# Two edits to a planned transformer kernel: K staged in bf16 before it is spread, and the last chunk worked in halves

## The chip, the cores and the metric

The kernel runs on one core of one Trainium2 chip. The metric is device time in microseconds for one launch; lower is better.

## The reference

Two layers with the same weights, each an attention block and a feed-forward block, over one sequence of 2048 rows of 512 in bf16:

```python
x = x + _A_ref(_layernorm(x), A_wqkv, A_wo)      # attention
x = x + _B_ref(_layernorm(x), B_w1, B_w2)        # feed forward
x = x + _A_ref(_layernorm(x), A_wqkv, A_wo)
x = x + _B_ref(_layernorm(x), B_w1, B_w2)

# _A_ref: H = 32 heads of Dh = 16, window W = 256
qkv = x @ wqkv                                    # 512 -> 3 x 512
scores = einsum("bhqd,bhkd->bhqk", q, k) * Dh ** -0.5
mask = (idx[:, None] - idx[None, :] >= 0) & (idx[:, None] - idx[None, :] < W)
o = softmax(where(mask, scores, -1e9)) @ v
return o @ wo
# _B_ref: relu(x @ w1) @ w2, 512 -> 1792 -> 512
```

## The kernel before

The 2048 rows are worked in chunks of 512, four for each layer: steps k = 0 to 7 (`NSTEP` is 8), counted layer by layer, so that k = 7 is the last chunk of the second layer. For each step there is:

- `plan_qkv(k)`: normalise four blocks of 128 rows, turn them (a DMA transpose, in step 0 TensorE), then K and Q for four groups t of 8 heads, and V for four blocks of rows.
- `plan_attention(k)`: scores, exp on ScalarE, masks on VectorE or GpSimd, P times V on TensorE (tile `acc`), division on VectorE into `O`. It goes by `Unit`s. A whole unit is one t with all 512 queries (8 blocks of 64); its scores are made in five groups of 2048 columns over four row groups (`FULL`). A half unit has 256 queries (4 blocks), and three groups, the last of half the width (`HALF`). All scores share one PSUM tile `Sps`, so a group's scores wait for the exp of the group before. `HALVED` lists the steps that are worked in half units: (0,).
- `plan_rest(k)`: turn `O` (a DMA transpose, in the last step TensorE), multiply by `wo`, add the residual, normalise, turn, then W1 with ReLU into `hT` (14 tiles f) and W2 for four blocks of rows. In a step of `HALVED`, W1 runs for 256 columns at a time, and W2 of the first two blocks stands between the two halves. There is one `hT` and one `xn2T`, so W1 of a step waits for W2 of the step before.

K is kept "spread" in `KBD`: for each slot of 64 keys two copies, one with the even heads' rows and one with the odd heads' rows, the other rows zero. `spread_k` writes it with two operations, each multiplying by a column of `par` (0 or 1 by the parity of the row's head). `KBD` is a ring of 20 slots; a chunk of 8 slots that runs over the ring's end (steps 2 and 7) takes four operations. Before the change `spread_k` reads the PSUM tile of the projection, on VectorE or ScalarE. V takes another way: it is copied from PSUM to a bf16 staging tile `Vst`, one of three buffers of the pool `stg`, and spread into `V2` from there on GpSimd or VectorE. The output tiles `ob` use `stg` too.

The order of all work is made ahead of time by a planner in the kernel's own Python (lines 692 to 800). Every operation has a key, the engines that may run it, and a planned time for each. The planner walks through time; when an engine is idle it takes the ready operation with the lowest key (on TensorE) or the lowest ready time plus key (elsewhere), and an operation that needs a buffer waits until one is planned to be free. Scores have the lowest keys of all. Projections are keyed by the score group ahead of which they are wanted: `at = first_slot[...] - 16`, sixteen groups early. W1 and W2 have later keys and fill TensorE between score groups. Where nothing can run, the planner puts a `warm` matmul on TensorE whose result nobody uses. Each engine then runs its operations in exactly the planned order, whatever the real times are. Four PSUM buffers (`psum`) serve all projections, transposes and `acc`.

Every instruction goes through one helper, so all carry the same line number (L106) in the profile, and groups are told apart by tile names: `KBD`, `Vst`, `Sps`, `Pb` (the exponentials), `acc`, `ps_d` (projections), `hT`, `xn`, `OT`.

Of the kernel before, what the change touches and what calls it, by code (L numbers as in the profile page):

```python
# [10 lines left out]
BF16 = mybir.dt.bfloat16  # L11
I32 = mybir.dt.int32
AX = mybir.AxisListType
ACT = mybir.ActivationFunctionType
ALU = mybir.AluOpType
P = 128
# [46 lines left out]
def kernel(  # L63
# [19 lines left out]
    NSTEP = 2 * NCH  # L83
# [31 lines left out]
    pe, dve, act, pool, sp = (InOrder(x) for x in (nc.tensor, nc.vector, nc.scalar, nc.gpsimd, nc.sync))  # L115
# [38 lines left out]
    par = const.tile([P, 2], FP32, name="par")  # L154
# [31 lines left out]
    SOON = {"qkv": 0, "v": 0, "h": 0, "mask": 0, "div": -1, "add": -1}  # L186
# [34 lines left out]
    def op(key, opts, deps=(), take=None, uses=(), keep=0):  # L221
        uses = list(uses) + ([take] if take is not None and take not in uses else [])
        return Op(key, opts, deps, take, uses, keep)
# [3 lines left out]
    stg = Pool("stg", 3, work)  # L227
# [11 lines left out]
    d_wo, d_w1 = landed(18.0), landed(24.0)  # L239


    def copy(e, o, i, relu=False):
        if e == "ACT":
            act.activation(o, i, ACT.Relu if relu else ACT.Copy)
        elif e == "POOL":
            pool.tensor_copy(o, i)
        elif relu:
            dve.tensor_relu(o, i)
        else:
            dve.tensor_copy(o, i)  # L250

    EVAC = {512: {"DVE": 0.67, "ACT": 0.59}, 256: {"DVE": 0.42, "ACT": 0.38}}

    def options(times, fn):
        return {e: (t, lambda e=e: fn(e)) for e, t in times.items()}
# [67 lines left out]
    def spread_k(e, layer, c, t, h0, h1, ps):  # L323
        s0 = slot(layer, 8 * c)
        for a, b in ([(h0, h1)] if s0 + h1 <= NSLOT or s0 + h0 >= NSLOT else [(h0, NSLOT - s0), (NSLOT - s0, h1)]):
            sa = (s0 + a) % NSLOT
            for p in range(2):
                o = KBD[:, t, sa:sa + b - a, p, :]
                i = ps[:, 64 * a:64 * b].rearrange("p (s k) -> p s k", k=64)
                if e == "ACT":  # L330
                    act.activation(o, i, ACT.Copy, scale=par[:, p:p + 1])
                else:
                    dve.tensor_scalar(out=o, in0=i, scalar1=par[:, p:p + 1], scalar2=None, op0=ALU.mult)

    def spread_v(e, layer, c, j, src):
        v4 = src.rearrange("p (a e d) -> p e a d", e=2, d=16)
# [80 lines left out]
        dve.tensor_tensor(out=x_sb[:, b, :], in0=ps, in1=x_raw(b, b + 1)[:, 0, :] if raw else x_sb[:, b, :], op=ALU.add)  # L417


    HALVED = (0,)  # L420
    units, base = [], []
    for k in range(NSTEP):
        base.append(sum(len(u.groups) for u in units))
# [12 lines left out]
    c_par = op(-9, {"DVE": (0.5, parity)}, [c_pidx])  # L436
# [15 lines left out]
    k_done, q_done, v_done, qkv_mm, w1_mm, w2_mm, x_done = {}, {}, {}, {}, {}, {}, {}  # L452
# [8 lines left out]
    def plan_qkv(k):  # L461
        layer, c = divmod(k, NCH)
        xnTs[k] = xnT = [None]
        src = [x_raw(4 * c + j, 4 * c + j + 1)[:, 0, :] if layer == 0 else x_sb[:, 4 * c + j, :] for j in range(4)]
        lid = 2 * k
        st, dst = [], []
        calm = (-10, 1, 40, 60)[k] if k < 4 else 0
        for j in range(4):
            came = [d_x[j // 2] if c == 0 else d_xc[c]] if layer == 0 else [x_done[k - 4, j]]
            st.append(norm_stats(lid, j, src[j], came + applied.get(lid - 8, []), j - 1 if j % 2 else None, calm))  # L470
        pw = [norm_pow(lid, j, j + 2, [st[j], st[j + 1]], calm - 5) for j in (0, 2)]
        free = [] if k == 1 else qkv_mm.get(k - 1, []) + (qkv_mm[0] if k == 2 else [])

        class Late:
            def __getitem__(self, i):
                if xnT[0] is None:
                    xnT[0] = work.tile([P, KC, 512], BF16, name="xnT", tag="hT" if k == 1 else "xnT", bufs=1)
                return xnT[0]
        for j in range(4):
            dst.append(norm_apply(lid, j, src[j], [pw[j // 2]], k == 0, Late(), -5000, free))  # L480
        applied[lid] = list(dst)
        mine = qkv_mm[k] = []
        old = [scores[s] for n in units_of.get(k - 2, []) for s in range(first_slot[n], first_slot[n] + len(units[n].groups))]
        old_pv = [pvs[n, j] for n in units_of.get(k - 2, []) for j in range(units[n].nq // 2)]
        wait = 0 if k == 0 else 16
        for h in range(2) if k == 0 else (None,):
            cols = slice(0, 512) if h is None else slice(256 * h, 256 * h + 256)
            h0, h1 = (0, 8) if h is None else (4 * h, 4 * h + 4)
            us = 0.216 if h is None else 0.115
            need_x = dst if h is None else dst[2 * h:2 * h + 2]  # L490
            w = 512 if h is None else 256
            for t in range(4):
                at = first_slot[units_of[k][t + 4 * (h or 0)]] - wait
                idx = 4 * k + t

                def kmm(kc, ps, t=t, cols=cols):
                    mm(ps[:, cols], wqkv[:, kc, D + t * P:D + (t + 1) * P], xnT[0][:, kc, cols], kc == 0, kc == KC - 1)
                box, m = group(at, KC, us, kmm, need_x + [d_w[1]] + old[len(old) * t // 4:len(old) * (t + 1) // 4], lead=1000)
                times = {"DVE": 1.46, "ACT": 1.42} if h is None else {"DVE": 0.87, "ACT": 0.83}
                k_done[k, t, h or 0] = op(SOON["qkv"], options(times, lambda e, t=t, h0=h0, h1=h1, box=box:  # L500
                                                      spread_k(e, layer, c, t, h0, h1, box.ps)),
                                          [m, c_par], None, [box])

                def qmm(kc, ps, t=t, cols=cols):
                    mm(ps[:, cols], wqkv[:, kc, t * P:(t + 1) * P], xnT[0][:, kc, cols], kc == 0, kc == KC - 1)
                last_use = [scores[s] for n, u in enumerate(units) if 4 * u.k + u.t == idx - 7
                            for s in range(first_slot[n], first_slot[n] + len(u.groups))]
                box, m2 = group(at + 0.1, KC, us, qmm, need_x + [d_w[0]] + last_use, lead=1000)

                def qev(e, t=t, cols=cols, box=box, idx=idx):  # L510
                    q = first(Q, (k, t), lambda: work.tile([P, 512], BF16, name="Qt", tag=f"Q{idx % 7}", bufs=1))
                    copy(e, q[:, cols], box.ps[:, cols])
                q_done[k, t, h or 0] = op(SOON["qkv"], options(EVAC[w], qev), [m2], None, [box])
                mine += [m, m2]
        for j in range(4):
            at = first_slot[units_of[k][0]] + (1 + (8 if j > 1 else 0) if k == 0 else 1.6 * j - wait)

            def vmm(kc, ps, j=j):
                mm(ps[:], xnT[0][:, kc, j * P:(j + 1) * P], wqkv[:, kc, 2 * D:3 * D], kc == 0, kc == KC - 1)
            box, m = group(at + 0.2, KC, 0.216, vmm, ([dst[j]] if k == 0 else dst) + [d_w[2]] + old_pv, lead=1000)  # L520
            vs = Box(stg)

            def vev(e, box=box, vs=vs):
                vs.t = vs.tile([P, 512], BF16, "Vst")
                copy(e, vs.t[:], box.ps[:])
            ev = op(SOON["qkv"], options(EVAC[512], vev), [m], vs, [box, vs])
            v_done[k, j] = op(SOON["v"], options({"POOL": 1.72, "DVE": 1.42} if k else {"POOL": 1.72, "DVE": 1.42, "ACT": 1.48}, lambda e, j=j, vs=vs: spread_v(e, layer, c, j, vs.t[:])),
                              [ev] + c_v, None, [vs])
            mine.append(m)
# [58 lines left out]
    def plan_rest(k):  # L588
# [43 lines left out]
        w1_mm[k], w2_mm[k] = [], []  # L632
        for j0, j1 in ((0, 2), (2, 4)) if k in HALVED else ((0, 4),):
            if k in HALVED:
# [78 lines left out]
    started, score_end, idle_since, log = set(), [0.0], [1.9], []  # L713
    score_next = [0]

    by_name = {"PE": pe, "ACT": act, "DVE": dve, "POOL": pool, "SP": sp}

    def choose(e, t):
        best = None
        for at, o in ready[e]:  # L720
# [39 lines left out]
    while events and events[0][0] < 3000:  # L760
        t, _, o, e = heapq.heappop(events)
# [15 lines left out]
        for e in ENGINES:  # L777
            if busy[e] > t + 1e-9:
                continue
            o = choose(e, t)  # L780
# [4 lines left out]
            elif e == "PE" and done_ops[0] < len(ops) - 12:  # L785
                if t - idle_since[0] >= (0.4 if t > 20 else 0.0) and sum(1 for f, _ in psum.free if f <= t) > 1:
                    box = Box(psum)
# [85 lines left out]
    with tc.If(flag > 0):  # L873
# [13 lines left out]
        for layer in range(2):  # L887
            for c in range(NCH):
# [3 lines left out]
                for t in range(4):  # L892
                    q = work.tile([P, 512], BF16, name="Qt", tag=f"Q{t}", bufs=1)
                    Qts.append(q)
                    whole(KC, lambda kc, ps: mm(ps[:], wqkv[:, kc, t * P:(t + 1) * P], xnT[:, kc, :], kc == 0, kc == KC - 1),
                          lambda ps: nc.vector.tensor_copy(q[:], ps[:]))
                    whole(KC, lambda kc, ps: mm(ps[:], wqkv[:, kc, D + t * P:D + (t + 1) * P], xnT[:, kc, :], kc == 0, kc == KC - 1),
                          lambda ps: spread_k("DVE", layer, c, t, 0, 8, ps))
                for j in range(4):
                    whole(KC, lambda kc, ps: mm(ps[:], xnT[:, kc, j * P:(j + 1) * P], wqkv[:, kc, 2 * D:3 * D], kc == 0, kc == KC - 1),  # L900
                          lambda ps: spread_v("DVE", layer, c, j, ps[:]))
# [52 lines left out]
```

## Time and profile before

| | |
|---|---|
| median of 3 runs | 484.27 us (484.21 to 484.54) |
| the profiled execution | 484.21 us, span 482.5 us |
| granted TensorE clock | 1.000 |
| PE busy | 461.9 us, 5935 matmuls |
| DVE (VectorE) busy | 366.4 us |
| ACT (ScalarE) busy | 337.2 us |
| POOL (GpSimd) busy | 312.4 us |
| score matmuls / exps | 1472 / 160 |

The span runs from the first to the last instruction; the time of an execution has some 1.7 us around it. A busy TensorE is not one at its peak, since the ends of matmuls are modelled: where matmuls of 512 columns stand back to back, each is shown with a duration of 0.38 us, but one starts every 0.216 us. The starts are what to count by.

### The profile page before, as it was taken

How to read it: one execution, taken by the hardware profiler on the slowest of the kernel's cores; microseconds unless marked ns; L12 is line 12 of the kernel's file. 1: busy time of each engine (PE TensorE's matmuls, PEld its weight loads, DVE VectorE, ACT ScalarE, POOL GpSimd, SP SyncE). 2: the span in 40 equal slices, each digit the busy share in tenths (PEclk: the TensorE clock that was granted, in tenths of full speed). 3: DMA queues.
4: the chain of work that ended last, by engine and by line, in shares of the span. 5: the costliest groups of instructions: out<-in, count | busy, mean ns of one | idle time of the engine just before them, and what ended most of it. 6: DMA issues, size and time to landing. Idle time of an engine off the chain costs nothing.

```text
span 482.5 us, 14414 instructions
## 1 busy us (share of the span) xinstructions
PE 461.9 (96%) x5935; PEld 242.3 (50%) x5935; DVE 366.4 (76%) x960; ACT 337.2 (70%) x268; POOL 312.4 (65%) x708
## 2 busy tenths in 40 slices
PE   7889899998899999999999999999999999999995
PEld 3555556654445545554544554455555545554442
DVE  6989899858897789878989977898758876473101
ACT  3877877877777767876778877777876787735240
POOL 7778878768876778777878767677655566520000
PEclk9999999999999999999999999999999999999999
DMA  8770231004300142002311023020153002000101
GB/s 271 244 206 3 45 45 25 2 3 67 67 1 3 24 67 46 3 1 45 58 34 33 13 35 47 12 46 1 24 89 57 13 1 56 24 14 12 35 12 37
DMA packets 54649, 21.98 MB, mean 46 GB/s; under 512 B 46128, under 2 KB 54064, under 8 KB 54576
## 3 DMA queue, kind: packets, MB, share of 16 engines
q1 hardware_dynamic: 54576, 20.98, 19.8%
q8 instruction: 48, 0.79, 0.7%
q14 instruction: 25, 0.20, 0.2%
HBM read 7.86 MB, written 2.10 MB: 21 GB/s over the span
## 4 chain that ended last, share of the span: by engine, by line
PE 72%; DVE 10%; DMA 7%; POOL 6%; issue 2%; ACT 2%; DVEq 0%; ACTq 0%; POOLq 0%
PE ps_d L106 52%; PE acc L106 12%; PE Sps L106 8%; DMA OT<-O 4%; POOL Pb L106 3%; ACT Pb L106 2%; DVE KBD L106 1%; DVE st L106 1%; DMA xn2T<-xn 1%; DVE xn L106 1%; DVE Pb L106 1%; POOL xn L106 1%; DVE x_sb L106 1%; DVE V2f L106 1%; DMA xnT<-xn 1%
## 5 line engine op out<-in xcount | busy, mean ns | idle before, releaser
L106 ACT ACTIVATE Pb<-Sps 128x2048 bf16<-128x2048 f32 (+4 forms) x160 | 283.3, 1770 | 94.4 <-PE Sps L106 75.8
L106 POOL TENSOR_SCALAR_AFFINE_SELECT Pb<-Pb 64x256 bf16<-64x256 bf16 x518 | 222.9, 430 | 99.3 <-ACT Pb L106 77.4
L106 PE MATMUL ps_d<-xn2T,w 128*128 128x512 bf16 (+1 forms) x504 | 109.5, 356 | 1.2 <-DVE hT L106 0.9
L106 PE MATMUL ps_d<-w,hT 128*128 128x512 bf16 x448 | 109.0, 380 | 0.0
L106 PEld LDWEIGHTS <-Pb 128*128 128x128 bf16 x2880 | 83.5, 96 | 25.6 <-issue 8.6
L106 PE MATMUL acc<-V2f,Pb 128*128 128x34 bf16 x2880 | 90.1, 178 | 2.3 <-POOL Pb L106 1.3
L106 PE MATMUL ps_d<-xnT,wqkv 128*128 128x512 bf16 (+1 forms) x288 | 66.5, 356 | 2.2 <-DMA xnT<-xn 1.0
L106 PEld LDWEIGHTS <-w 128*128 128x128 bf16 x504 | 45.3, 97 | 44.7 <-issue 5.4
L106 PE MATMUL Sps<-Qt,KBD 32*128 32x192 bf16 (+4 forms) x1472 | 61.6, 252 | 2.8 <-ACT Pb L106 2.5
L106 PEld LDWEIGHTS <-hT 128*128 128x128 bf16 x448 | 40.3, 98 | 46.0 <-issue 3.6
L106 DVE TENSOR_TENSOR Pb<-Pb,tri 128x512 bf16<-128x512 bf16 (+1 forms) x136 | 58.8, 437 | 5.0 <-ACT Pb L106 4.6
L106 DVE TENSOR_SCALAR hT<-ps_d 128x512 bf16<-128x512 f32 (+1 forms) x74 | 45.8, 625 | 11.4 <-PE ps_d L106 10.9
L106 PEld LDWEIGHTS <-KBD 32*128 32x128 bf16 x1472 | 24.0, 92 | 51.7 <-issue 48.9
L106 DVE TENSOR_SCALAR KBD<-ps_d,par 128x256 bf16<-128x256 f32 (+1 forms) x82 | 45.5, 604 | 1.6 <-PE ps_d L106 1.5
L106 DVE BATCH_NORM_STATS2 st<-x_sb 128x6 f32<-128x512 f32 (+1 forms) x64 | 43.7, 683 | 0.9 <-DMA x_sb<-in_A_x_dram 0.6
L106 ACT ACTIVATE hT<-ps_d 128x512 bf16<-128x512 f32 (+1 forms) x52 | 28.4, 550 | 20.9 <-PE ps_d L106 19.4
L106 DVE TENSOR_TENSOR x_sb<-ps_d,x_sb 128x512 f32<-128x512 f32 x48 | 32.7, 684 | 13.0 <-PE ps_d L106 12.4
L106 DVE TENSOR_TENSOR O<-acc,chk 128x128 bf16<-128x128 f32 x128 | 37.3, 291 | 4.5 <-DMA OT<-O 0.2
L106 DVE RECIPROCAL chk<-acc 128x8 f32<-128x8 f32 x128 | 25.6, 200 | 17.7 <-PE acc L106 15.2
L106 PEld LDWEIGHTS <-wqkv 128*128 128x128 bf16 x288 | 25.7, 97 | 26.1 <-issue 4.0
L106 DVE TENSOR_TENSOR ob<-ps_d,x_sb 128x512 bf16<-128x512 f32 x16 | 11.0, 690 | 34.4 <-PE ps_d L106 34.3
L106 PE MATMUL ps_d<-wo,OT 128*128 128x512 bf16 x128 | 32.5, 380 | 3.9 <-DMA OT<-O 3.6
(55 smaller groups left out, 300.3 us busy)
## 6 DMA issues: line engine op xcount, KB each, us to landing
w<-in_B_w_dram SPq DMA_DIRECT2D x2, 1792.0 KB, 10.0
out_dram<-ob SPq DMA_DIRECT2D x16, 128.0 KB, 1.7
wqkv<-in_A_wqkv_dram SPq DMA_DIRECT2D x3, 512.0 KB, 7.0
x_sb<-in_A_x_dram SPq DMA_DIRECT2D x3, 512.0 KB, 8.9
x_sb<-in_A_x_dram SPq DMA_DIRECT2D x2, 256.0 KB, 2.9
wo<-in_A_wo_dram SPq DMA_DIRECT2D x1, 512.0 KB, 8.9
xnT<-xn SPq DMA_TRANSPOSE x28, 2.5
OT<-O SPq DMA_TRANSPOSE x28, 2.5
```

Source lines behind the costliest of these rows:

```text
L106: inst = fn(*a, **k)
```

## The change

Two edits. `HALVED` gets the last step, so the last chunk's attention is done in half units and its W1 and W2 in halves of 256 queries. And in steps 1 to 7 K is first copied from PSUM to a bf16 staging tile `Kst` of the pool `stg` (on VectorE or ScalarE), and spread into `KBD` from there, on VectorE or GpSimd, with planned times of 0.8 and 1.3 us. Step 0 still spreads K from PSUM in halves. The change's short description also names a later load of W2; the line that plans that load is the same in both kernels.

```diff
@@ spread_k
                 if e == "ACT":
                     act.activation(o, i, ACT.Copy, scale=par[:, p:p + 1])
                 else:
-                    dve.tensor_scalar(out=o, in0=i, scalar1=par[:, p:p + 1], scalar2=None, op0=ALU.mult)
+                    by_name[e].tensor_scalar(out=o, in0=i, scalar1=par[:, p:p + 1], scalar2=None, op0=ALU.mult)
...
-    HALVED = (0,)
+    HALVED = (0, NSTEP - 1)
...
                 times = {"DVE": 1.46, "ACT": 1.42} if h is None else {"DVE": 0.87, "ACT": 0.83}
-                k_done[k, t, h or 0] = op(SOON["qkv"], options(times, lambda e, t=t, h0=h0, h1=h1, box=box:
-                                                      spread_k(e, layer, c, t, h0, h1, box.ps)),
-                                          [m, c_par], None, [box])
+                if k == 0:
+                    k_done[k, t, h or 0] = op(SOON["qkv"], options(times, lambda e, t=t, h0=h0, h1=h1, box=box:
+                                                                   spread_k(e, layer, c, t, h0, h1, box.ps[:])),
+                                              [m, c_par], None, [box])
+                else:
+                    ks = Box(stg)
+
+                    def kev(e, box=box, ks=ks):
+                        ks.t = ks.tile([P, 512], BF16, "Kst")
+                        copy(e, ks.t[:], box.ps[:])
+                    ev = op(SOON["qkv"], options(EVAC[512], kev), [m], ks, [box, ks])
+                    k_done[k, t, 0] = op(SOON["qkv"], options({"DVE": 0.8, "POOL": 1.3}, lambda e, t=t, ks=ks:
+                                                              spread_k(e, layer, c, t, 0, 8, ks.t[:])),
+                                         [ev, c_par], None, [ks])
```

The table `by_name` (engine name to engine) moves up so that `spread_k` can use it. A fallback path that did not run here gets a matching edit.

More of the change, by code (lines that the diff above doesn't have):

```diff
@@ L239 @@
     d_wo, d_w1 = landed(18.0), landed(24.0)
+    by_name = {"PE": pe, "ACT": act, "DVE": dve, "POOL": pool, "SP": sp}
     def copy(e, o, i, relu=False):
@@ L714 @@
     score_next = [0]
-    by_name = {"PE": pe, "ACT": act, "DVE": dve, "POOL": pool, "SP": sp}
     def choose(e, t):
@@ L897 @@
                     whole(KC, lambda kc, ps: mm(ps[:], wqkv[:, kc, D + t * P:D + (t + 1) * P], xnT[:, kc, :], kc == 0, kc == KC - 1),
-                          lambda ps: spread_k("DVE", layer, c, t, 0, 8, ps))
+                          lambda ps: spread_k("DVE", layer, c, t, 0, 8, ps[:]))
                 for j in range(4):
```

## The prediction

> **What bounds it now.** I read the page's parts 1 and 2 first, then busy time by stage, then the chain of waits, then the groups by shape.
>
> ```profile
> PE 461.9 (96%) x5935; PEld 242.3 (50%) x5935; DVE 366.4 (76%) x960; ACT 337.2 (70%) x268; POOL 312.4 (65%) x708
> ...
> core 0: us, PE busy (x) PEld busy (x) DVE busy (x) ACT busy (x) POOL busy (x), PEclk, DMA share, GB/s
> 24.00:104.00 80.00, 75.79 (x1156) 45.50 (x1157) 70.36 (x196) 62.41 (x52) 62.98 (x144) 1.00 0.22 50
> 104.00:126.00 22.00, 19.47 (x267) 9.82 (x264) 18.07 (x54) 16.15 (x11) 17.32 (x40) 1.00 0.30 50
> 126.00:400.00 274.00, 269.60 (x3726) 138.70 (x3723) 228.49 (x577) 208.58 (x144) 196.24 (x448) 1.00 0.18 31
> 400.00:428.00 28.00, 28.00 (x391) 15.13 (x388) 15.69 (x46) 19.05 (x15) 15.94 (x35) 1.00 0.16 40
> 428.00:453.00 25.00, 25.00 (x130) 11.86 (x129) 10.96 (x27) 8.85 (x15) 1.83 (x3) 1.00 0.05 17
> ```
>
> PE sets the end. From 126 us on it stands idle for only 4.4 us (274.00 less 269.60). Earlier it loses 4.2 us in 24 to 104 and 2.5 in 104 to 126, and it fills some of the rest with useless `warm` matmuls: 8 near 50 us, 8 in 104 to 126, at 0.216 us about 3.5 us in all. So about 10 us can be won before 126 us and about 4 after it; the rest is matmul time.
>
> The end of the chain shows why the last chunk has nothing to wait for:
>
> ```profile
> 443.10 34.33 PE ps_d L106 x159
> 477.43 0.02 issue
> 477.45 0.69 DVE ob L106
> ```
>
> 159 matmuls at 0.216 us stand back to back. The last attention matmul is at 426.1 us, and behind it lie most of W1 and all of W2 of chunk 6, then both for chunk 7.
>
> The one place where the K spread is on the chain:
>
> ```profile
> 108.23 1.56 DVE KBD L106 x4
> ...
> 110.62 1.56 DVE KBD L106 x4
> ...
> 113.68 3.90 DMA OT<-O
> 117.59 0.05 issue
> 117.63 1.05 PE ps_d L106 x4
> ```
>
> DVE spreads two K tiles of chunk 2 before the divisions whose result the transpose waits for, and PE then runs 5 warm matmuls and stands idle for 1.2 us. These are the prices:
>
> ```profile
> L106 DVE TENSOR_SCALAR KBD<-ps_d,par 128x512 bf16<-128x512 f32 x40 | 28.0, 741 | 0.9 <-PE ps_d L106 0.9
> L106 DVE CAST Vst<-ps_d 128x512 bf16<-128x512 f32 x18 | 12.3, 684 | 0.9 <-PE ps_d L106 0.7
> L106 ACT ACTIVATE Vst<-ps_d 128x512 bf16<-128x512 f32 x14 | 8.3, 595 | 0.5 <-PE ps_d L106 0.2
> L106 DVE TENSOR_SCALAR xn<-x_sb,mvs,rstds 128x512 bf16<-128x512 bf16 x10 | 4.2, 440 | 1.5 <-POOL rstds L106 1.5
> L106 POOL TENSOR_SCALAR xn<-x_sb,rstds,nbs 128x512 bf16<-128x512 bf16 x6 | 5.0, 836 | 0.6
> ```
>
> **The change, part by part.** The profiled execution took 484.21 us (span 482.5 and 1.7 around it), 0.06 below the median of 484.27, so I add to the median.
>
> *Scores of the last chunk.* A whole unit has five groups of 512 columns. Two half units have four of 512 and two of 256. In the chain a group of 8, 12 or 16 score matmuls of 512 columns takes 0.33 us, one of 4 takes 0.22 (at 41.96 us), and the ten matmuls ahead of a group take 2.26 instead of 2.16, so 0.10 more a group. That is 5 x 0.43 = 2.15 against 4 x 0.43 + 2 x 0.32 = 2.36: 0.21 for each of four t, **+0.84 us** on PE, which has no gap there to hide it.
>
> *W1 of the last chunk.* 112 matmuls of 256 columns replace 56 of 512. Chunk 0 already runs that shape: 14 in 1.54 us (62.00 to 63.54), 0.110 each. The 56 take 12.09 us (453.08 to 465.17); 112 x 0.110 = 12.32: **+0.2 us**. The 28 extra evictions (0.415 us on DVE, 0.381 on ACT) keep up: PE needs 0.44 us for each half tile and two engines share them. Nothing.
>
> *Earlier start of the first half: nothing.* Its W1 still waits for W2 of chunk 6 (one `hT`), and that ends at 453 us. Feed-forward work already fills PE during attention. The attention itself grows: a small group costs about 0.22 + 1.02 (its exp) + 0.37 of handover, 1.61, against 2.59 for a full one, so 2 x (2 x 2.59 + 1.61) = 13.6 against 13.0 us, 2.4 us for four t. What hides it: normalised rows are turned by 443 us and wanted at 453. Without that cover it would cost 2.4.
>
> *K, 28 tiles (chunks 1 to 7).* DVE pays 1.40 us a tile now (two of 0.741, 0.66 apart), 1.56 where the ring of slots wraps (four of 0.475). Afterwards: a copy (0.684 DVE or 0.595 ACT) and two spreads from bf16. No row shows such a spread. On DVE I take 0.44 each, the bf16 normalisation (its extremes are 0.384 and 0.578; the freest bf16 copy, half as wide, takes 0.22). On POOL 0.80, between 0.77 and 0.84. So DVE pays from nothing (ACT and POOL) to 1.56 (all DVE) a tile; at half and half 0.34 + 0.44 = 0.78, a gain of 0.6 or a little more. That is 17 us of DVE, but DVE isn't the bound after 126 us. On the chain it is worth 2 x 0.6 near 110 us; the ends are zero and the dry time of 104 to 126, 2.5 + 1.7 = 4.2. I take **-1.0**, since not all of PE's wait there is DVE's. A PSUM buffer comes free 0.7 us sooner; the waits for KBD that it could shorten are about 2 us, the most of them in that place or under it: nothing more. The scores want K sixteen groups later, so the longer way to KBD is covered; without that cover it adds about 1.5 us once a chunk.
>
> *POOL and the queues behind it.* The planner enters 1.3 us for a spread on POOL; I expect 1.6. What is queued behind it are masks, PV waits for the masks, and PE takes its work in order. 14 such spreads, 0.3 late each, are 4.2 us; POOL has 99 us of idle before masks, and PE's waits on POOL masks now total about 5 us. I take a quarter, **+1.0**; the ends are zero and 4.2. Every instruction after the first K copy of chunk 1 (31 us) is also ordered anew, so the 4.4 us of single waits after 126 are dealt again: 0, with 2 us either way. Three staging buffers now serve K as well as V: eight uses a chunk in place of four, each of a few us, in 30 us or more; nothing. W2's load, named in the description, isn't touched by the diff: nothing.
>
> Sum: +0.84 + 0.2 - 1.0 + 1.0 = **+1.0, 485.3 us**.
>
> A copy beside a busy POOL is the second thing that can shift these prices:
>
> ```profile
> L106 DVE COPY V2f<-Vst x64: 217/434/468, 13.2 to 382.5; 64x256 bf16<-64x256 bf16 x64
> L106 POOL COPY V2f<-Vst x64: 392/399/690, 14.5 to 381.4; 64x256 bf16<-64x256 bf16 x64
> ```
>
> The same DVE copy takes 217 ns at best and 434 at the median, and POOL's takes up to 690 against 399; the spread from PSUM stays between 717 and 751 ns. The Trainium skill ("SBUF — State Buffer", Who interferes with whom) says that a DVE instruction using both ports, SBUF to SBUF, and a GpSimd one exclude each other for their whole length; by that rule the new spread is exposed where the old was not, and the trace's doubled copies agree. By it some 28 spreads on DVE would each hold POOL or be held for about 0.2 us (434 less 217), 5.6 in all and a quarter of it at PE, and the sum would be 486.7 in place of 485.3. In "VectorE: DVE Perf Modes" (Rules for kernel authors) it advises copying PSUM to SBUF first where several operations follow; no run here shows whether two are enough.
>
> **Rivals.** *Relief on DVE is worth all of the dry time* (28%): spreads cost 0.22 to 0.3 us, or go to POOL without harm, and the transposes of O start 3 us earlier near 113 us. For: DVE is busy 88% in 24 to 104 and the chain runs through KBD. Against: POOL is at 79% there too and takes the work. It gives 484.3 + 1.0 - 4.2 = 481.1 at its end (without POOL's lateness), 482.2 in the middle.
> *POOL's masks come late* (25%): the 0.3 us of each spread, and exclusion beside DVE, reach PE through the masks. It decides from about half of the 14 spreads on, 2.1 us. At its end 484.3 + 1.0 + 4.2 = 489.5 without relief, 487.5 in the middle.
> *The planner gives POOL none* (5%): copy and spreads stay on DVE, 1.56 for 1.40; PE's +1.0 remains: 485.4.
> *The forecast* (42%): relief and lateness cancel, PE's +1.0 is left; 484.2 to 486.5.
>
> **Numbers.** A measurement of this kernel tells about 0.2% (0.97 us) from no change, so 483.3 to 485.2 is the same. Faster: the first rival, 0.28. Same: the lower half of the forecast's range and of the third rival, 0.24. Slower: the upper halves and the second rival, 0.48. The range for 8 in 10 leaves out the last of the relief and of the lateness: 481.3 to 488.6.
>
> **What would show it.** Sps matmuls rise from 1472 to 1536 and exps from 160 to 164; 224 W1 matmuls of 256 columns. 28 Kst copies, DVE spreads near 0.44 us, POOL's near 0.8. DVE busy falls by over 10 us, POOL's rises by some 20. PE stays back to back from 443 us to the end. I am wrong if that tail shows gaps, if idle before 126 us falls by 3 us or more, or if PE's waits on POOL masks double.

## The result, and the profile after

The changed kernel takes 492.63 us (median of four runs, 491.66 to 493.60) against 484.35 for the kernel before on the same chip: ratio 1.0171, 95% interval 1.015 to 1.0191. It is slower by 8.3 us, where 1.0 was forecast, and lies outside the range. The profiled execution took 491.66 us, with a span of 489.6 against 482.5.

Busy time by stage, in the same columns as for the kernel before:

```profile
24.00:104.00 80.00, 71.35 (x1043) 42.53 (x1044) 65.78 (x187) 58.61 (x50) 69.28 (x137) 0.98 0.22 49
104.00:126.00 22.00, 18.23 (x292) 9.89 (x289) 15.61 (x47) 16.60 (x10) 17.40 (x36) 1.00 0.28 38
126.00:400.00 274.00, 269.76 (x3689) 139.18 (x3689) 228.21 (x609) 210.24 (x152) 200.32 (x437) 1.00 0.19 32
```

Most of TensorE's added idle time lies in 24 to 104 us: PE stands idle for 8.65 us in place of 4.2, while POOL is busy for 69.3 in place of 63.0 and VectorE for 65.8 in place of 70.4. From 104 to 126 PE's idle time is 3.8 in place of 2.5. After 126 it did not grow (4.2 against 4.4), although POOL is busier there too (200.3 against 196.2), and PE stands back to back to the end as before. The mean clock of the first stage is 0.98.

One place holds most of it. The chain of waits there (start, duration, what):

```profile
51.75 6.47 POOL KBD L106 x4
58.21 0.70 POOL rstds L106
...
59.60 0.76 POOL xn L106
...
60.94 0.76 POOL xn L106
61.70 0.69 POOL rstds L106
62.39 0.03 issue
62.42 0.96 DVE xn L106 x2
63.37 0.34 DVE hT L106
63.71 0.04 issue
63.75 1.01 PE ps_d L106 x4
```

Four spreads, two K tiles of chunk 1, occupy POOL for 6.47 us where the plan has 2 x 1.3 = 2.6, so POOL is 3.9 us late behind them. Behind them in POOL's order stand the powers of two normalisations (`rstds`). VectorE's next operation in its order, a normalisation, waits for the second power; behind it stand the evictions of `hT`, and behind those a PSUM buffer that PE waits for. POOL, VectorE and TensorE stand in line behind the spreads. The list of waits puts it as (who <- for whom: us in total, times, longest):

```profile
DVE xn L106 <- POOL rstds L106: 6.8, 3, 5.3
...
PE ps_d L106 <- DVE hT L106: 4.4, 1, 4.4
```

The longest of each, 5.3 us of VectorE and 4.4 of PE, is this one. Right behind it the clock falls (the number before the last two is the granted TensorE clock):

```profile
62.00:64.00 2.00, 0.25 (x2) 0.18 (x2) 1.58 (x5) 0.00 (x0) 1.85 (x5) 0.91 0.47 91
64.00:66.00 2.00, 2.00 (x42) 1.45 (x40) 1.59 (x7) 0.00 (x0) 1.77 (x5) 0.50 0.58 111
66.00:68.00 2.00, 2.00 (x37) 1.68 (x30) 1.83 (x7) 1.73 (x1) 0.84 (x3) 0.74 0.47 94
```

The shares missing from full clock in the three rows, 0.09 x 2 + 0.50 x 2 + 0.26 x 2 = 1.7 us, are 3.4 us at half clock if the clock was half or full (the middle row has 0.50), and cost up to 1.7 us more. The account of the 7.1 us of span is then: 4.4 of idle before 104 us, 1.2 in 104 to 126, about 1.0 of added matmul time (an estimate from the prediction's rows), up to 1.7 for the clock, less about 0.65 since three warm matmuls fewer were made (35 for 38), and less 0.5 of idle before 24 us.

The new operations, by tile (min, median and max in ns):

```profile
L106 DVE TENSOR_SCALAR KBD<-Kst,par x48: 272/442/703, 43.7 to 398.7; 128x512 bf16<-128x512 bf16 x32, 128x256 bf16<-128x256 bf16 x16
L106 POOL TENSOR_SCALAR KBD<-Kst,par x24: 920/986/1897, 33.5 to 393.6; 128x256 bf16<-128x256 bf16 x16, 128x512 bf16<-128x512 bf16 x8
```

and by shape:

```profile
L106 POOL TENSOR_SCALAR KBD<-Kst,par 128x256 bf16<-128x256 bf16 x16 | 15.5, 988 | 0.1
L106 DVE TENSOR_SCALAR KBD<-Kst,par 128x512 bf16<-128x512 bf16 x32 | 14.1, 480 | 0.1
L106 POOL TENSOR_SCALAR KBD<-Kst,par 128x512 bf16<-128x512 bf16 x8 | 13.3, 1676 | 0.3
```

A spread of 512 columns takes POOL 1.68 us, not the 0.80 that I took from the normalisation of the same shape. Eight tiles went to POOL (four whole, four over the ring's end), 28.8 us in all where the plan holds 10.4.

### The profile page after: what moved, and what is told of

Same layout as the page of the kernel before. It is cut to its first block, busy times and chain, and to the rows that moved or that the text cites. A ratio compares the mean times of both kernels' runs of the same rounds, so it can differ in the third digit from the quotient of the medians.

```text
span 489.6 us, 14698 instructions
## 1 busy us (share of the span) xinstructions
PE 463.9 (95%) x6052; PEld 249.8 (51%) x6052; DVE 365.4 (75%) x992; ACT 343.9 (70%) x290; POOL 328.8 (67%) x699
## 4 chain that ended last, share of the span: by engine, by line
PE 70%; POOL 15%; DMA 5%; DVE 4%; ACT 3%; issue 3%; POOLq 0%; ACTq 0%; DVEq 0%
PE ps_d L106 51%; PE acc L106 11%; PE Sps L106 8%; POOL Pb L106 7%; DMA OT<-O 4%; POOL KBD L106 3%; ACT Pb L106 3%; POOL V2f L106 1%; POOL xn L106 1%; POOL rstds L106 1%; DVE V2f L106 1%; POOL nbs L106 1%; DMA x_sb<-in_A_x_dram 1%; DMA xnT<-xn 1%; DVE st L106 1%
## 5 line engine op out<-in xcount | busy, mean ns | idle before, releaser
L106 PE MATMUL ps_d<-xn2T,w 128*128 128x512 bf16 (+1 forms) x560 | 110.9, 338 | 4.9 <-DVE hT L106 4.4
L106 PEld LDWEIGHTS <-Pb 128*128 128x128 bf16 x2880 | 84.2, 96 | 28.8 <-issue 9.3
L106 PE MATMUL acc<-V2f,Pb 128*128 128x34 bf16 x2880 | 91.1, 178 | 4.7 <-POOL Pb L106 3.1
L106 PEld LDWEIGHTS <-w 128*128 128x128 bf16 x560 | 51.1, 98 | 42.8 <-issue 8.3
L106 DVE TENSOR_TENSOR Pb<-Pb,tri 128x512 bf16<-128x512 bf16 (+1 forms) x143 | 59.2, 421 | 10.2 <-ACT Pb L106 9.8
L106 DVE TENSOR_SCALAR hT<-ps_d 128x512 bf16<-128x512 f32 (+1 forms) x77 | 47.0, 615 | 10.8 <-PE ps_d L106 10.0
L106 PEld LDWEIGHTS <-KBD 32*128 32x128 bf16 x1536 | 25.5, 92 | 51.3 <-issue 47.0
L106 ACT ACTIVATE hT<-ps_d 128x256 bf16<-128x256 f32 (+1 forms) x63 | 30.0, 478 | 23.0 <-PE ps_d L106 21.3
L106 DVE TENSOR_TENSOR x_sb<-ps_d,x_sb 128x512 f32<-128x512 f32 x48 | 32.6, 684 | 14.9 <-PE ps_d L106 14.7
L106 PE MATMUL ps_d<-wqkv,xnT 128*128 128x512 bf16 x128 | 34.1, 379 | 0.1
```

The costliest lines, as they stand in the source:

```text
L106: inst = fn(*a, **k)
```

## The experiments

The theory: POOL's spread takes 3.2 to 4.2 us a tile, the planner books 1.3, and what is queued behind it on POOL comes late to an order that can't move. The rivals: the halves cost the time; three staging buffers are too few for K and V; VectorE's bf16 form suffers beside POOL; K itself comes late to the scores. Ratios are to the kernel before, run beside each on the same chip, with 95% intervals.

### One part at a time

The halves alone, in the kernel before:

```diff
-    HALVED = (0,)
+    HALVED = (0, NSTEP - 1)
```

> The kernel before with the last chunk in halves, K still spread from PSUM. Theory (the loss is K's spread on POOL, 1.6 us an instruction where 0.65 was planned): only the added score groups count, +0.8 to +1.2 us, about 485.4. Rival (the halves cost the time, by smaller matmuls and a longer attention): 490 or more. No spread on POOL, so no stall of over 2 us after 40 us.

Measured: 485.94 us, ratio 1.001 (0.9994 to 1.0027): 0.5 us, between -0.3 and +1.3. Score matmuls rose to 1536 and exps to 164 as they must. The halves are not the loss.

K staging alone, in the changed kernel:

```diff
-    HALVED = (0, NSTEP - 1)
+    HALVED = (0,)
```

> The changed kernel with the last chunk whole: K staging alone. Theory: nearly all of the loss, 490 to 492 us, with the stall of over 4 us near 59 us and half the TensorE clock for some 3.4 us behind it, since the plan is the same up to the last chunk's projections. Rival (halves): about 484 to 485.

Measured: 499.42 us, ratio 1.0287 (1.0259 to 1.0316). The loss is here, as expected, but it is larger without the halves, by 1.2%, which neither theory had. The list of PE's waits shows where:

```profile
PE ps_d L106 <- DMA OT<-O: 4.7, 4, 2.6
PE ps_d L106 <- DVE hT L106: 4.3, 1, 4.3
PE Sps L106 <- POOL KBD L106: 3.8, 2, 2.1
PE acc L106 <- POOL Pb L106: 3.2, 5, 0.9
```

The stall by way of `hT` is the same. New is the third row: twice PE stands for about 2 us before scores that need the tile POOL is spreading, at 394 and 421 us, in the last chunk. So K coming late, one of the rivals, is real there, and is a second effect of the same slow spread. With the halves, the last spread on POOL starts at 390.9 us and not at 417.6, and the changed kernel has no such wait of that length.

The clock can make up the rest. In this profile PE works at half clock for 5.0 us behind the stall (63.7 to 68.7) and for another 3.4 behind a wait of 2.65 us near 126 us, 8.4 in all against 3.4 in the changed kernel: up to 2.5 us more. 3.8 and 2.5, less the 1.0 of matmul time that the halves would add, is 5.3, and the two spans differ by 5.2 (494.8 and 489.6). The changed kernel has the same wait near 126 us, 2.7 long, and no half clock behind it.

### The spread off POOL, or at its true price

```diff
-options({"DVE": 0.8, "POOL": 1.3}, ...)
+options({"DVE": 0.8}, ...)
```

> The changed kernel, with the spread of K from the staging tile on VectorE alone (GpSimd is taken off the list of engines). Theory (POOL's spread): 484 to 486.5, no stall of over 2 us near 59 us, granted clock back to 1.000. Rival (three staging buffers shared by K and V): staging stays as tight as it is, so 490 or more. Rival (DVE slowed by the bf16 form beside POOL): 488 or more, DVE busier by 5 us than in the kernel before.

Measured: 482.87 us, ratio 0.996 (0.9937 to 0.9983). Not only is the loss gone, it is faster than the kernel before by 1.9 us (0.8 to 3.1), staging buffers and halves as in the changed kernel. So neither the staging buffers nor the bf16 form on VectorE is the cause. VectorE's busy time didn't rise:

```profile
PE 464.2 (97%) x6058; PEld 249.9 (52%) x6058; DVE 364.2 (76%) x1000; ACT 344.4 (72%) x292; POOL 308.5 (64%) x689
```

364.2 us against 366.4, with all 28 spreads on it. K costs it 41.6 us (25.5 for the spreads, 10.2 for its share of the copies, 5.9 for chunk 0) where it cost 45.5, and V's copies 27.9 where they cost 23.7.

```diff
-options({"DVE": 0.8, "POOL": 1.3}, ...)
+options({"DVE": 0.9, "POOL": 3.3}, ...)
```

> The changed kernel, with the planned times of the spread set to what the trace shows: 0.9 us for two on VectorE and 3.3 for two on GpSimd, in place of 0.8 and 1.3. Theory (the wrong planned time, not POOL's work as such, makes the loss): the planner still gives POOL some tiles but knows when they end; 484 to 487. Rival (any spread on POOL costs, planned or not, as it takes time from the masks): 489 or more if POOL keeps as many tiles.

Measured: 483.68 us, ratio 0.9965 (0.9948 to 0.9982). POOL still does four tiles, as slow as ever:

```profile
L106 POOL TENSOR_SCALAR KBD<-Kst,par x12: 920/1026/2091, 33.6 to 376.7; 128x256 bf16<-128x256 bf16 x8, 128x512 bf16<-128x512 bf16 x4
```

but the planner knows when each ends. It also gives POOL half as many tiles as in the changed kernel and none where the stall was, near 52 us, so the right price takes work off POOL as well as placing what is left; this run doesn't part the two. The next one helps: there POOL does five tiles, 16.5 us against 14.7 here, at the wrong price, and the kernel is 0.9% slower than before in place of 0.35% faster. That speaks for the price more than for the slow operation, in two different orders of work.

### Where the lateness bites

Chunk 1 alone off POOL:

```diff
+options({"DVE": 0.8} if k == 1 else {"DVE": 0.8, "POOL": 1.3}, ...)
```

> The changed kernel, with the spread taken off GpSimd for chunk 1 alone; later chunks keep the planned 1.3 us and 3.2 us real. Theory: the stall of 4.5 us near 59 us and the half clock behind it go, and PE waits less before the transposes of chunk 2; 486 to 489, some 4 to 6 us less than the changed kernel. Rival (lateness adds up evenly over all tiles on POOL): only the share of chunk 1, less than 2 us, is won, 490 or more.

Measured: 488.66 us, ratio 1.009 (1.0075 to 1.0106). The stall near 59 us is gone, and about half of the loss with it (1.7% to 0.9%, some 3.9 us). The rest sits elsewhere, in an order that is new from chunk 1 on: in this profile one tile on POOL from 198.5 to 201.8 us delays the masks behind it, and PE waits 3.0 us for them up to 205.6 us. The profiled execution is the fastest of the four (485.99 us at a mean clock of 1.000; the others took 488.1 to 489.2 at 0.990 to 0.994), so it shows only a part of the rest.

Lateness without any work of K, in the kernel with all spreads on VectorE:

```diff
+if k == 1 and t == 3:
+    for _ in range(5):
+        pool.tensor_tensor(out=extra[:], in0=extra[:], in1=mhalf[:, 0:2], op=ALU.pow)
```

> The kernel with all spreads on VectorE, and five operations of about 0.72 us on GpSimd that the planner doesn't know of and nobody waits for, put where the spread of chunk 1's last tile stands: 3.6 us of pure lateness, no work of K. Theory (what is queued behind on POOL makes the loss: the power for the normalisation, then the masks): TensorE stands idle some 3 to 5 us near 55 to 62 us, and the total is 3 to 6 us above the kernel without them, 486 to 489. Rival (K coming late to the scores makes the loss, not POOL's queue): within 1 us of the kernel without them.

Measured: 486.45 us, ratio 1.0039 (1.0022 to 1.0057), against 0.996 without the five operations: about 0.8%, 3.8 us (roughly 2.4 to 5.2, from the two intervals). The chain and the waits around it:

```profile
51.40 0.74 POOL extra L106
...
54.53 0.69 POOL extra L106
55.22 0.38 POOL Pb L106
55.60 0.06 issue
55.65 0.43 POOL Pb L106
56.08 0.05 issue
56.13 0.50 PE acc L106 x11
```

```profile
PE acc L106 <- POOL Pb L106: 4.4, 2, 4.1
DVE xn L106 <- POOL rstds L106: 4.1, 1, 4.1
```

Here it comes through two masks instead of the power, PE stands for 4.1 us, and the clock falls to half as well. 3.8 us that the planner doesn't know of (51.40 to 55.2), put on POOL at this place, cost about as much as they last, the clock included. That shows the mechanism without K.

### Why POOL's spread is slow

Six forms on POOL behind the work of the kernel before, in one row of 512 bf16:

```diff
+pool.tensor_scalar(out=flat, in0=src, scalar1=par[:, 0:1], scalar2=None, op0=ALU.mult)
+pool.tensor_scalar(out=ring, in0=src3, scalar1=par[:, 0:1], scalar2=None, op0=ALU.mult)
+pool.tensor_scalar(out=flat, in0=src, scalar1=par[:, 0:1], scalar2=par[:, 1:2], op0=ALU.mult, op1=ALU.add)
+pool.tensor_scalar(out=ring, in0=src3, scalar1=par[:, 0:1], scalar2=par[:, 1:2], op0=ALU.mult, op1=ALU.add)
+pool.tensor_copy(flat, src)
+pool.tensor_copy(ring, src3)
```

> The kernel before, with six forms of a 128x512 bf16 operation on GpSimd put behind its last planned work, three times each: one factor or factor and addend, and a plain copy, each into a flat row and into runs of 64 with gaps of 64 (as in KBD). Theory A (the gaps cost): both forms with gaps take about 1.57 us and the flat ones 0.77. Theory B (the form with one operation costs): the one-factor forms take 1.57 flat and with gaps, the two-operation forms 0.77. Neither: all near 0.77, and the slow spread comes from its neighbours on VectorE. Total within 1 us of before plus what of the 18 instructions stands after TensorE's end.

The second round, in order of time (start, us), in the order of the lines above:

```profile
441.21 1.55 POOL L106 TENSOR_SCALAR Pb<-Pb,par 128x512 bf16<-128x512 bf16 x1
442.75 1.55 POOL L106 TENSOR_SCALAR Pb<-Pb,par 128x512 bf16<-128x512 bf16 x1
444.29 0.76 POOL L106 TENSOR_SCALAR Pb<-Pb,par 128x512 bf16<-128x512 bf16 x1
445.04 0.76 POOL L106 TENSOR_SCALAR Pb<-Pb,par 128x512 bf16<-128x512 bf16 x1
445.75 0.60 POOL L106 COPY Pb<-Pb 128x512 bf16<-128x512 bf16 x1
446.30 0.61 POOL L106 COPY Pb<-Pb 128x512 bf16<-128x512 bf16 x1
```

Theory B holds: a multiplication alone takes twice as long as a multiplication and an addition, and runs with gaps cost nothing. The third round agrees within 0.01 us; in the first the two one-factor forms took 1.71 and 1.74. Why the shorter form is the slower one is not shown. The total was 484.41 us, in a single execution. So the changed kernel with an addition of zero behind the multiplication, and nothing else:

```diff
-scalar2=None, op0=ALU.mult
+scalar2=None if e == "DVE" else 0.0, op0=ALU.mult, op1=ALU.add   # op1 on GpSimd alone
```

> The changed kernel, whose spread on GpSimd adds 0.0 behind the multiplication; planned times, plan and order are the same. Theory (one operation costs 1.55 us there, two 0.76, and the lateness against the planned 1.3 makes the loss): 1.5 us a tile in place of 3.2, no stall of over 2 us near 59 us, 482 to 486. Rival (any K on POOL harms the masks): 488 or more.

Measured: 484.59 us, ratio 1.0004 (0.999 to 1.0019), from the same plan as the changed kernel.

```profile
L106 POOL TENSOR_SCALAR KBD<-Kst,par x24: 468/529/885, 33.6 to 385.4; 128x256 bf16<-128x256 bf16 x16, 128x512 bf16<-128x512 bf16 x8
```

The same 24 spreads, in about half the time, and the 8 us are gone. PE's idle time from 56 to 66 us is 1.65 us (8.35 busy of 10) where the changed kernel has 4.45.

### Better versions

Last chunk whole again, with the spread on VectorE alone, run twice; with POOL at 3.3 us; and with the added zero at 1.55 us on POOL (VectorE's price at 0.9 in these two):

> Spread from the staging tile on VectorE alone and the last chunk whole. Theory (halves cost about 0.9 us of TensorE): 0.5 to 1.5 us under the same kernel with halves, so 481.5 to 482.5. Rival (the new order decides more than 1 us of matmul time): anywhere within 3 us of it, on either side.

> The kernel with all spreads from the staging tile on VectorE and the last chunk whole, once more beside the others on one chip. Theory: ratio to before 0.993 to 0.997 as in its first run. Nothing in it tells theories apart; it is the mark for the other three.

> One operation on GpSimd as in the changed kernel, but planned at 3.3 us, 0.9 on VectorE, last chunk whole. Theory: as with halves, less their 0.5 to 1 us: 481.5 to 483.5. Rival (K on POOL comes late to the scores of the last chunk where that is whole): a stall of 2 us or more before scores after 380 us, 486 or more.

> The same spread with an added 0.0, planned at 1.55 us on GpSimd and 0.9 on VectorE, and the last chunk whole. Theory: the planner places what the chip then does; 480.5 to 483, at or under the best so far. Rival (order decides more than the terms): 484 or more.

Measured: 481.95 us (0.9946, 0.9933 to 0.996) and 482.23 (0.9949, 0.9932 to 0.9966); 482.35 (0.9954, 0.9935 to 0.9973); 482.67 (0.9955, 0.9934 to 0.9975). All three versions beat both kernels by 0.45 to 0.55% over the kernel before, 2.2 to 2.6 us, and can't be told from each other. The halves cost about 0.1% by the comparison of kst_dve with its whole twin, and the intervals overlap.

## Why the prediction was wrong

The direction was right, and so was the engine: POOL's queue comes late, as the second rival has it. The path was right in part. The prediction let the lateness reach PE through masks alone; PE's matmuls did wait more for them (3.1 us against 1.3, and its weight loads 6.6 against 3.3, so its sign *if PE's waits on POOL masks double* came true), but the 4.4 us went by a power, a normalisation and `hT`. The prediction's own row for VectorE's normalisation has this wait, 1.5 us behind `rstds`. The step that failed is the term *POOL and the queues behind it*: "The planner enters 1.3 us for a spread on POOL; I expect 1.6." It measured 3.3 us a whole tile and 3.9 on average where the ring wraps (2 x 1.676 and 4 x 0.988).

- The price came from the row of POOL's normalisation, same shape and type, 0.77 to 0.84. That row has two operations and the spread has one; pool_forms shows 0.76 against 1.55. Both bounds of my 0.80, "between 0.77 and 0.84", are the fastest and the mean of that one form, although the prediction itself says that no row shows such a spread.
- "14 such spreads, 0.3 late each": eight tiles, 2.3 late each (18.4 us over 8). The total lateness was 18.4 us, not 4.2, and the quarter of it that I let reach PE, 4.6, would have given 488.9, still under the 492.6. The rest is that one place, chunk 1, passes on nearly all of its 3.9, and the clock. The error of the price decided: pool_two has the same plan with the spreads 13.7 us in all, 3.3 over the planned 10.4 and so near the 4.2 that I assumed, and it measured 484.6, within the range.
- *The clock* was in no step. All three profiles with a stall of over 4 us (the changed kernel, kst_only, late_pool) have half clock behind or around it.
- *The longer way to KBD is covered*: this held in the changed kernel, but was wrong where the last chunk is whole: 3.8 us in kst_only. Sixteen groups ahead is when the projection is keyed, not when it runs.
- *Relief on DVE*, -1.0: K's staging without POOL and without the halves measured -2.6 us (kst_dve_whole, -1.9 to -3.2), more than the term. It isn't VectorE's time that makes it, for in kst_dve that fell by 2 us in all. There PE's idle time is lower by 2.0 us in 126 to 400 (2.4, 274.00 less 271.59, against 4.4), for which I entered 0 with 2 us either way, and by 0.8 in 24 to 104; near 110 us it is lower by 0.4 only. Whether the earlier free PSUM buffer does this, or ACT's share of the copies, or just another order, wasn't tried and stays open.
- *VectorE's spread at 0.44 us* held (0.48 mean at 512 columns).
- *Scores of the last chunk* and *W1*, +1.04: 0.5 us measured, -0.3 to 1.3, and 56 W1 matmuls of 256 columns take 6.1 us (472.10 to 478.21), 0.109 each. The tail stood back to back, and the earlier start brought nothing, as argued.
- DVE was to lose over 10 us and POOL to gain some 20: POOL gained 16.4, but DVE lost only 1.0: K costs it 12 us less, and the planner moved V's spreads to it (88 V copies on DVE in place of 64, 7.5 us more) and other work.
- The exclusion rule of the Trainium skill ("SBUF — State Buffer", Who interferes with whom), by which the sum would have been 486.7: the bf16 spread does lengthen beside POOL (in kst_dve, at 512 columns, 333 to 354 ns in the four cases where POOL is idle, 500 at the median beside it, up to 703), but with every spread on VectorE the kernel is faster than before, so it didn't decide. The advice of the Trainium skill ("VectorE: DVE Perf Modes", Rules for kernel authors) to copy out of PSUM first agrees with kst_dve_whole, which is faster by 1.9 to 3.2 us with one copy for two operations; that the copy as such makes the gain is not shown.

## What to carry to other kernels

In a kernel whose order is planned ahead, a wrong duration can cost more than a slow operation: with the slow spread at its true price the kernel gained 0.35% (the planner then gave POOL half as many tiles), with it at 40% of that price it lost 1.7%. Price a new operation from its own form (engine, number of operations, operands), and if no row has that form, keep a factor of two in the range. Look at what stands behind the operation on its engine, above all small operations that another engine's order hangs on, such as the power of a normalisation.

## What the runs showed of the hardware

On GpSimd a tensor_scalar with one operation took 1.55 us for 128x512 bf16, with two operations 0.76, and a copy 0.60, flat or in runs of 64. Adding a zero halves the time. On VectorE no such thing shows: one operation took 0.33 to 0.70 us for the same shape, and the two operations of the normalisation 0.38 to 0.58.

The TensorE clock fell to half in three profiles with a stall of over 4 us. In the changed kernel it fell 4.3 us after PE's last work, for 3.4 us; in kst_only, at the same stall, after 2.5, for 6.8; in late_pool after 1.3, for 6.8 (0.95, 0.50 and 0.65 granted in 48 to 54, 54 to 56 and 56 to 62 us). A shorter wait can do it too: near 120 us it fell behind a wait of 2.1 us in kst_true and of 2.3 in kst_dve_whole, both faster than the kernel before. The same wait near 126 us was followed by half clock in kst_only (2.65 us) and not in the changed kernel (2.7). The Trainium skill ("TensorE: Matmul & The Clock Gate", Part 1: The HAM clock gate) states half rate after an idle window of about 3.4 us. The lengths of 3.4 and twice that fit such a window, and so does the changed kernel's stall; the waits of 1.3 to 2.65 us before the fall do not, so in this case no stall length can be named that is safe or that is sure to cost the clock.
